# A list of instructions ordered by new ranks: lengths of ScalarE's pieces, ranks of pairs and weights' pieces, and an output tile of its own for the last half

## The chip, the cores and the metric

The kernel runs on 1 core of one Trainium2 chip. The metric is the device time of one execution in microseconds (us), lower is better. The engines are named PE (TensorE, matmuls), DVE (VectorE), ACT (ScalarE), POOL (GpSimd) and SP (SyncE, which here only issues DMAs).

## What is computed

Block-causal attention over 8 batches of 8 heads, 576 positions and 64 features, and behind it a gated feed-forward layer on all 4608 tokens. Cut to what matters:

```python
# q, k, v: (8, 8, 576, 64); blocks of 64 positions, a query sees its own and earlier blocks
scores = q @ k.transpose(0, 1, 3, 2) / sqrt(64)
scores = where(block_i >= block_j, scores, -1e9)
attn = exp(scores - scores.max(-1, keepdims=True))
attn = attn / (attn.sum(-1, keepdims=True) + 1e-9)
x = (attn @ v).transpose(0, 2, 1, 3).reshape(4608, 512)
g = x @ w_gate                       # (512, 1536)
out = (g * sigmoid(g) * (x @ w_val)) @ w_out      # (1536, 512), fp32 out
```

The weights arrive as 64-bit floats, as two 32-bit words each.

## The kernel before

**The work and its pieces.** The attention goes by pairs of heads: four pairs to a batch. Batches 0 and 1 are cut into tokens 0 to 255 and 256 to 575 (the table FIRST), so that the feed-forward of the first 256-token tiles can begin early; later batches go whole. For one pair PE makes scores (L429 for the first two batches after transposes L403; L555 with operands in high and low parts for the others, whose low part DVE makes at L523). ACT copies scores out of PSUM (L447, L473, L565) and hides what a block may not see (L452, L470). DVE takes the maximum over keys (L603), POOL reduces it over partitions (L607), DVE subtracts it (L631), ACT takes the exponential (L635), and PE multiplies with v (L675). In batch 0 DVE divides at once, out of PSUM (L702 to L709).

A feed-forward tile holds 256 tokens. Every value goes as a high and a low part, so that each product is three matmuls: L998 to L1000 for gate and value (into PSUM tiles gv), L1089 to L1091 for the output (into po or at). Between them ACT takes a tanh (L1031), DVE multiplies (L1034, L1039), ACT makes the high part (L1044) and DVE the low one (L1047). At a tile's end ACT copies the sums out (L1116) and SP stores them. In the very last 128 tokens the row is halved: DVE copies the second half (L1114), and ACT's queue stores it.

The weights come in 36 pieces (12 of each of w_gate, w_val, w_out). Each is loaded into one of five buffers wo, turned from 64-bit to 32-bit words by ACT and DVE (L857, L861, L866, L871), and split into a high part by ACT (L876) and a low part by DVE (L879).

**What sets the order.** Nothing is issued where it is written. `add(engine, cost, rank, fn, after, bufs)` records a task with an estimated length, a rank, what it comes after, and the buffers it needs. When all tasks are recorded, `in_order` (L1184 and below) goes through them as a list scheduler does: each engine takes, of the tasks that are ready, the one with the lowest rank, if its buffers can be had; `spare` says how long before an engine is free a buffer may have come free. A task's end follows from its cost, so the costs decide the order too. The tasks are then issued in the order found, and each engine works its own line strictly in that order. The times in the scheduler are estimates of its author and appear nowhere else.

The ranks are numbers written out by hand: PIECES (one for each piece of the weights), AHEAD (for the loads of the first pieces), FIRST (pairs of the first two batches), LEAD (how far ahead of the feed-forward a later batch goes), SIDE (the first two feed-forward tiles), EAGER (how far the scores go ahead of the rest of a pair) and MIXED (how the sixths of the first two tiles follow each other). `act_us` gives the cost of a piece of ACT's work, 0.08 us and 0.000833 us for each column.

Of the kernel before, what the change touches and what calls it, by code (L numbers as in the profile page):

```python
# [18 lines left out]
def kernel(  # L19
# [19 lines left out]
    NT, DM = out.shape  # L39
# [3 lines left out]
    TB = 96  # L43
# [6 lines left out]
    XT = 256  # L50


    LEAD, EAGER = 1.88, 0.3

    SUMS = 2

    MIXED = (0, 0, 0, 1, 1, 0, 1, 0, 1, 0, 1, 1)

    FINE = 4

    AHEAD = {(0, 1): 2.01, (0, 2): 2.03, (1, 0): 2.5, (1, 1): 2.07, (1, 2): 2.07}
    LATER = 0.6

    PIECES = [
        (2.64, 2.64, 2.71),
        (2.85, 3.37, 2.76),
        (5.12, 5.12, 4.37),
        (4.66, 4.68, 4.68),
        (2.95, 3.91, 4.11),
        (4.18, 4.18, 4.91),  # L70
        (4.71, 4.38, 4.79),
        (2.20, 2.82, 2.82),
        (1.32, 1.14, 0.01),
        (1.91, 1.85, 2.33),
        (0.26, 1.61, 0.56),
        (2.08, 2.78, 1.84),
    ]

    SIDE = (3.40, 10.26)

    PATIENCE = 10.0

    FIRST = {
        0: [(0, 256, (2.02, 2.21, 2.06, 2.08)), (256, 576, (1.99, 2.09, 0.10, 2.03))],
        1: [(0, 256, (1.33, 2.46, 3.26, 3.40)), (256, 576, (1.79, 1.87, 2.05, 2.09))],
    }
    TILES = [XT] * (NT // XT)

# [70 lines left out]
        return t  # L159


    def act_us(n):
        return 0.08 + n * 0.000833

    def dve_us(n, one=False):
        return 0.07 + n * (0.00052 if one else 0.00104)
# [167 lines left out]
    def attention(R, b, h, a, e, early, bufs, lane):  # L334
# [1 line left out]

        Q = R - (0.001 if early else EAGER)
        visits, runs = STRETCHES[a, e]  # L340
        if b < 2:

# [27 lines left out]
        def plain_scores():  # L370
# [21 lines left out]
            for i in range(2):  # L392
                ps = Buf("gv") if whole else Buf("at", also=banks)
                nb = len(blocks[i])
                per = nb if nb < 6 else 3

                def turned(ps=ps):
                    return ps[0].rearrange("p (x n) -> p x n", x=1) if whole else ps[0]

                def transposes(i=i, turned=turned, per=per):  # L400
                    for m, c in enumerate(blocks[i]):
                        o = m % per * TB
                        nc.tensor.transpose(  # L403
                            turned()[:, m // per, o : o + TB],
                            qk[0][:TB, lane * 3 + c, 2 * i * D : 2 * (i + 1) * D],
                            ident[:TB, :TB],
                        )

                def out_of_psum(i=i, turned=turned, nb=nb, per=per):
                    o = L + blocks[i][0] * TB  # L410
                    nc.scalar.mul(
                        prt[i][:, o : o + nb * TB].rearrange("p (x n) -> p x n", x=nb // per),
                        turned()[:, 0 : nb // per, 0 : per * TB],
                        1.0 if i else SCALE,
                    )

                tr = add("PE", 0.083 * nb, R, transposes, [ld[i]], [qk, ps, prt])
                ready.append(add("ACT", act_us(nb * TB), R, out_of_psum, [tr], [ps, prt]))

            for visit in visits:  # L420
                both = [Buf("at", also=banks) for _ in visit]
# [18 lines left out]
                for parts, ps in zip(visit, both):  # L440
                    gw = sum(w for _, _, w in parts)
                    mixed = [(c, sum(w for _, _, w in parts[:i])) for i, (c, qs, _) in enumerate(parts) if qs == c * P]

                    def out_of_psum(parts=parts, ps=ps, gw=gw):
                        c, qs, _ = parts[0]
                        o = place[c] + qs - first[c]
                        nc.scalar.copy(sc[0][:, :, o : o + gw], ps[0][:, :, 0:gw])  # L447

                    def hide(mixed=mixed, ps=ps):

                        for c, o in mixed:
# [12 lines left out]

                    if whole:
                        stays.append(ps)

                        def hide_there(ps=ps):
                            x = ps[0].rearrange("p x (n w) -> p x n w", w=2 * P)[:, :, :, 0:BLK]
                            nc.scalar.activation(x, x, AF.Identity, bias=unseen)  # L470

                        def max_there(ps=ps):
                            nc.scalar.copy(mx[0][:, :, L : L + W], ps[0][:, :, 0:W])  # L473

                        t = add("ACT", act_us(4 * BLK) + 0.1, Q, hide_there, [pr], [ps])
                        t = add("ACT", act_us(2 * W), Q, max_there, [t], [ps, mx])
                        evac[0].append(t)
                        evac[1].append(t)
                        continue
                    t = add("ACT", act_us(2 * gw), Q, out_of_psum, [pr], [ps, sc])  # L480
                    if mixed:
                        t = add("ACT", 0.28 * len(mixed), Q, hide, [t], [ps, sc])
                    if parts[0][:2] == (0, 0):
                        t = add("ACT", 0.46, Q, first_max, [t], [ps, mx])
                    for c, _, _ in parts:
                        evac[c].append(t)

        def split_scores():
# [48 lines left out]
            for x in range(2):  # L537
                for group in (((0, 0, half), (0, half, half)), ((1, 4), (2, 3))):
# [42 lines left out]
                    t = add("ACT", act_us(2 * gw), Q, out_of_psum, [pr], [ps, sc])  # L581
# [105 lines left out]
        for i, s0, s1, _ in pieces:  # L687

            def out_of_psum(i=i, s0=s0, s1=s1):
                nc.scalar.copy(xu[0][:, L + s0 + here - a : L + s1 - a], ps[0][:, i, here : s1 - s0])  # L690

            if s1 - s0 > here:
                ends.append(add("ACT", act_us(s1 - s0 - here), R, out_of_psum, [pr], [ps, xu]))

        if here:
            xt, xhl = Buf("xt"), Buf("xhl")
# [14 lines left out]
            t = add("DVE", 1.2, 1.0, invert, [pr], [ps, sr, xt])  # L711
# [54 lines left out]
        if direct:  # L766
# [4 lines left out]
            sm = [add("ACT", act_us(W - here), R, sums_there, [pr], [ps, sr])] * 2  # L771
# [40 lines left out]
    def weight(i, kind):  # L812
# [68 lines left out]
            )  # L881

        if wide:
            t = add("ACT", act_us(DM), R, signs, [t], [raw, y])
            f = add("DVE", dve_us(DM), R, fraction, [t], [raw, y], True)
            t = add("ACT", act_us(DM), R, scaled, [t], [raw])
            t = add("DVE", dve_us(DM), R, exponent, [t, f], [raw], True)
        t = w_high[i, kind] = add("ACT", act_us(DM), R, high, [t], bufs)
# [75 lines left out]
    def feed_forward(j, t0, w, xs):  # L964
# [50 lines left out]
        for i in range(0, NFC, 2):  # L1015
# [32 lines left out]
                    hh[1][:, 0:n], t[0][:, 0:n], hh[0][:, 0:n].bitcast(F32), ALU.subtract  # L1048
                )

            a = add("ACT", act_us(n), E, tanh, [tg], [pg, t])
            a = add("DVE", dve_us(n), E, silu2, [a], [pg, t])
            a = add("DVE", dve_us(n), E, gated, [a, tv], [pv, t])
            a = add("ACT", act_us(n), E, high, [a], [t, hh])
# [48 lines left out]
                yield  # L1103

        for m in range(nb):
            ob = Buf("ob", "out")

            halves = 2 if ends_alone and m == nb - 1 else 1
            for x in range(halves):
                cols = slice(x * DM // halves, (x + 1) * DM // halves)  # L1110

                def out_of_psum(m=m, ob=ob, x=x, cols=cols):
                    if x:
                        nc.vector.tensor_copy(ob[0][:, cols], sums(m)[:, cols])  # L1114
                    else:
                        nc.scalar.copy(ob[0][:, cols], sums(m)[:, cols])  # L1116
# [5 lines left out]
                us = (dve_us if x else act_us)(DM // halves)  # L1122
# [61 lines left out]
    def in_order():  # L1184
# [14 lines left out]
        now = queue = 0.0  # L1199
        mode, last = "", None  # L1200

        spare = {"PE": 2.0, "DVE": 0.3, "ACT": 0.3, "POOL": 0.0, "SP": 0.0}

        def place(t, by):

# [104 lines left out]
```

## Time and profile before

| what | us |
|---|---|
| median of 3 runs (1180.5 to 1184.99) | 1183.08 |
| the profiled execution, its own time | 1180.03 |
| span in the profile | 1178.2 |
| PE busy | 1148.2 |
| DVE busy | 768.9 |
| ACT busy | 635.9 |
| POOL busy | 324.9 |

An engine's busy time is that of its instructions; register, branch, semaphore and DMA-issuing ones aren't counted. Matmuls are pipelined, so one lasts longer (0.28 us for 256 columns) than the step from its start to the next one's start, which is what the sums use. A row of a wait names the waiting engine and line, what it waited for, and then total us, times and longest. A wait for several things is put down to the one that came last.

### The profile page before, as it was taken

Reading aid. Unit: us, or ns where it says so; the run is one execution under the profiler, and the core shown is the slowest. Engines: PE = TensorE matmul, PEld = TensorE weight load, DVE = VectorE, ACT = ScalarE, POOL = GpSimd, SP = SyncE. Lnnn points to the kernel's source line nnn. Section 1 sums busy time; section 2 is a strip of 40 time slices with the busy share of each in tenths; the row PEclk is TensorE's granted clock in tenths of the full one; section 3 lists DMA queues with packets and bytes.
Section 4 is the critical chain, followed back from the end, with each engine's and each line's share of the span. In section 5 each row is a group of like instructions: output and inputs, shape, how many; then the busy total and the mean of one; then the engine's idle time right before and its main releaser. Section 6 shows DMA issues by size and latency. Waiting matters only on the chain.

```text
span 1178.2 us, 21734 instructions
## 1 busy us (share of the span) xinstructions
PE 1148.2 (97%) x8464; PEld 1029.9 (87%) x8464; DVE 768.9 (65%) x1234; ACT 635.9 (54%) x1150; POOL 324.9 (28%) x138
## 2 busy tenths in 40 slices
PE   6889999999999999999999999999999999999998
PEld 4667777889898989898998999898989899999997
DVE  5998988876687667877585767675767633323222
ACT  6898967757574736574655556564746312212111
POOL 3122110143634162345233325243344300000000
PEclk9999999999999999999999999999999999999999
DMA  8778656755564746755656464646662445453432
GB/s 214 188 199 214 192 180 197 208 178 160 147 169 115 210 146 176 204 164 153 181 168 182 138 192 134 198 134 190 159 199 92 153 157 183 150 167 136 144 130 103
DMA packets 266983, 197.40 MB, mean 168 GB/s; under 512 B 195264, under 2 KB 231376, under 8 KB 266880
## 3 DMA queue, kind: packets, MB, share of 16 engines
q1 hardware_dynamic: 264304, 195.29, 56.8%
q8 instruction: 66, 1.08, 0.4%
q10 hardware_dynamic: 2576, 0.72, 0.3%
q14 instruction: 37, 0.30, 0.1%
HBM read 171.57 MB, written 24.38 MB: 166 GB/s over the span
## 4 chain that ended last, share of the span: by engine, by line
PE 84%; ACT 6%; DVE 5%; DMA 2%; POOL 1%; issue 1%; SPq 0%; ACTq 0%; DVEq 0%; POOLq 0%
PE gv L998 15%; PE gv L1000 15%; PE gv L999 15%; PE po L1089 7%; PE po L1090 7%; PE po L1091 7%; PE at L555 7%; PE at L675 7%; POOL mx L607 1%; DVE mx L603 1%; DVE sc L631 1%; ACT sc L447 1%; ACT ob L857 1%; ACT sc L635 1%; DVE wo L866 1%
## 5 line engine op out<-in xcount | busy, mean ns | idle before, releaser
L607 POOL PARTITION_ALL_REDUCE mx<-mx x80 | 144.6, 1855 | 405.7 <-DVE mx L603 192.6
L998 PE MATMUL gv<-xhl,v_all 128*128 128x256 f32 x864 | 241.5, 280 | 0.7 <-DVE t L1039 0.7
L1000 PE MATMUL gv<-xhl,v_all 128*128 128x256 f32 x864 | 239.4, 277 | 0.0
L999 PE MATMUL gv<-xhl,v_all 128*128 128x256 f32 x864 | 239.3, 277 | 0.0
L726 POOL PARTITION_ALL_REDUCE mx<-mx x48 | 178.1, 3758 | 205.8 <-DVE mx L603 205.8
L1034 DVE SCALAR_TENSOR_TENSOR t<-t,gv 128x512 f32<-128x512 f32 x108 | 74.0, 685 | 209.3 <-ACT t L1031 208.9
L998 PEld LDWEIGHTS gv<-xhl,v_all 128*128 128x128 f32 x864 | 162.1, 188 | 4.9 <-issue 2.7
L999 PEld LDWEIGHTS gv<-xhl,v_all 128*128 128x128 f32 x864 | 162.3, 188 | 0.9
L1000 PEld LDWEIGHTS gv<-xhl,v_all 128*128 128x128 f32 x864 | 162.2, 188 | 0.0
L1031 ACT ACTIVATE t<-gv 128x512 f32<-128x512 f32 x108 | 64.5, 598 | 169.5 <-PE gv L1000 169.4
L1089 PE MATMUL po<-wo,hhl 128*128 128x512 f32 x372 | 147.7, 397 | 0.3 <-ACT ob L1116 0.3
L1090 PE MATMUL po<-wo,hhl 128*128 128x512 f32 x372 | 145.6, 391 | 0.0
L1091 PE MATMUL po<-wo,hhl 128*128 128x512 f32 x372 | 145.1, 390 | 0.0
L1044 ACT CAST hhl<-t 128x512 fp32r<-128x512 f32 x108 | 67.2, 622 | 139.3 <-DVE t L1039 138.0
L631 DVE TENSOR_TENSOR sc<-sc,mx 128x640 f32<-128x640 f32 (+6 forms) x168 | 123.9, 773 | 18.5 <-POOL mx L607 18.3
L635 ACT ACTIVATE sc<-sc 128x1024 f32<-128x1024 f32 (+3 forms) x104 | 105.5, 1028 | 35.8 <-DVE sc L631 35.1
L998 PE MATMUL gv<-xhl,g_even 128*128 128x256 f32 x432 | 123.2, 285 | 0.1
L999 PE MATMUL gv<-xhl,g_even 128*128 128x256 f32 x432 | 122.3, 283 | 0.2 <-DVE xhl L326 0.2
L1000 PE MATMUL gv<-xhl,g_even 128*128 128x256 f32 x432 | 122.1, 283 | 0.0
L1039 DVE SCALAR_TENSOR_TENSOR t<-t,gv 128x512 f32<-128x512 f32 x108 | 73.9, 684 | 73.1 <-PE gv L1000 72.7
L998 PE MATMUL gv<-xhl,g_odd 128*128 128x256 f32 x432 | 120.7, 279 | 0.7 <-ACT g_odd L876 0.7
L1000 PE MATMUL gv<-xhl,g_odd 128*128 128x256 f32 x432 | 119.7, 277 | 0.6 <-DVE g_odd L879 0.6
(157 smaller groups left out, 2465.2 us busy)
## 6 DMA issues: line engine op xcount, KB each, us to landing
wo<-wo_d SPq DMA_DIRECT2D x200, 512.0 KB
out_dram<-ob SPq DMA_DIRECT2D x35, 256.0 KB
v<-in_v_dram SPq DMA_DIRECT2D x64, 128.0 KB
xt<-x_d SPq DMA_DIRECT2D x64, 128.0 KB
rt<-r_d SPq DMA_DIRECT2D x128, 64.0 KB
qk<-in_q_dram SPq DMA_DIRECT2D x112, 72.0 KB
qk<-in_k_dram SPq DMA_DIRECT2D x104, 72.0 KB
x_d<-xu SPq DMA_DIRECT2D x24, 288.0 KB
```

The lines of the kernel that those rows point to most:

```text
L555: nc.tensor.matmul(ps[0][:, i, o : o + w], lhsT=prt[x][1][:, c * P : (c + 1) * P], rhs=m, start=not low, stop=low == 1,)
L607: nc.gpsimd.partition_all_reduce(m, m, channels=P, reduce_op=bass_isa.ReduceOp.max)
L631: nc.vector.tensor_tensor(piece(c), scores_of(c), m, ALU.subtract)
L635: nc.scalar.activation(x, x, AF.Exp)
L675: nc.tensor.matmul(ps[0][own(x), 1 - i if sums else i, q0 - s0 : s1 - s0], lhsT=ones if sums else vt[0][:, 2 * lane + c, own(x)], rhs=sc[0 ...
L726: nc.gpsimd.partition_all_reduce(m, m, channels=P, reduce_op=bass_isa.ReduceOp.add)
L998: nc.tensor.matmul(o, lhsT=hi[:, d], rhs=xhi[:, 0:w], start=first, stop=False)
L999: nc.tensor.matmul(o, lhsT=hi[:, d], rhs=xlo[:, 0:w], start=False, stop=False)
L1000: nc.tensor.matmul(o, lhsT=lo[:, d], rhs=xhi[:, 0:w], start=False, stop=last)
L1089: nc.tensor.matmul(po, lhsT=hi, rhs=whi, start=i + y == 0, stop=False)
L1090: nc.tensor.matmul(po, lhsT=hi, rhs=wlo, start=False, stop=False)
L1091: nc.tensor.matmul(po, lhsT=lo, rhs=whi, start=False, stop=i + y == NFC - 1)
```

## The change

Three kinds of edits. The cost of an ACT piece gets other numbers: 0.093 us in place of 0.08, 0.05 where it reads PSUM, and something more for three kinds of weights' work; DVE's `invert` and ACT's `hide` get other costs too. The hand-written ranks get other values (all of PIECES, AHEAD, FIRST; also LEAD, SIDE, MIXED, the early EAGER, and `spare`). And the second half of the last 128 tokens takes a buffer of tag t instead of sharing the one of tag ob. What is computed, with which instructions and shapes, stays as it is. Of the tables two lines stand for all:

```diff
-    LEAD, EAGER = 1.88, 0.3
+    LEAD, EAGER = 1.85, 0.3
-    MIXED = (0, 0, 0, 1, 1, 0, 1, 0, 1, 0, 1, 1)
+    MIXED = (0, 0, 0, 1, 1, 0, 0, 1, 1, 1, 0, 1)
     PIECES = [
-        (2.08, 2.78, 1.84),
+        (-6.75, -4.32, -5.69),
...
-    def act_us(n):
-        return 0.08 + n * 0.000833
+    def act_us(n, psum=False, more=0.0):
+        return (0.05 if psum else 0.093) + n * 0.000833 + more
...
-        Q = R - (0.001 if early else EAGER)
+        Q = R - (0.1 if early else EAGER)
...
         for m in range(nb):
-            ob = Buf("ob", "out")
 
             halves = 2 if ends_alone and m == nb - 1 else 1
             for x in range(halves):
+                ob = Buf("t") if x else Buf("ob", "out")
...
-        spare = {"PE": 2.0, "DVE": 0.3, "ACT": 0.3, "POOL": 0.0, "SP": 0.0}
+        spare = {"PE": 1.59, "DVE": 0.30, "ACT": 0.75, "POOL": 0.0, "SP": 0.0}
```

What moves is seen in the lines of the engines. First, ACT at the start of the program: loads of k (qk), the load of its function tables (L1142), copies of transposed q and k (parts), and the first scores (at) and their copy (mx). Before:

```order
L1142 ACT_TABLE_LOAD
L1142 ACTIVATE seen<-seen 128x1
L379 DMA qk_0_124<-in_k_dram 96x3x64 x2
L379 DMA qk_0_127<-in_k_dram 96x3x64 x4
L411 ACTIVATE parts_0_148<-gv_0_138 128x288
L379 DMA qk_0_124<-in_k_dram 96x3x64 x2
L411 ACTIVATE parts_1_149<-gv_0_154 128x288
L470 ACTIVATE at_0_164<-at_0_164,unseen 128x4x64
L411 ACTIVATE parts_0_148<-gv_0_138 128x288
L473 COPY mx_0_178<-at_0_164 128x2x256
```

Now:

```order
L379 DMA qk_0_123<-in_k_dram 96x3x64 x2
L1142 ACT_TABLE_LOAD
L1142 ACTIVATE seen<-seen 128x1
L379 DMA qk_0_133<-in_k_dram 96x3x64 x4
L379 DMA qk_0_123<-in_k_dram 96x3x64 x2
L411 ACTIVATE parts_0_155<-gv_0_142 128x288
L411 ACTIVATE parts_1_156<-gv_0_148 128x288
L470 ACTIVATE at_0_164<-at_0_164,unseen 128x4x64
L473 COPY mx_0_174<-at_0_164 128x2x256
L411 ACTIVATE parts_0_155<-gv_0_142 128x288
```

Two loads went ahead of the table load, two ahead of the first L411, and L473 ahead of the next pair's L411.

Second, DVE at one of the maxima in batch 1 (sc_0_291 the scores of a pair, mx_0_245 or mx_0_241 their maximum, which POOL reduces between the last L603 and the first L631; wo and g are weights). Before:

```order
L879 TENSOR_TENSOR wo_0_1572<-wo_0_96,wo_0_1572 128x512
L603 TENSOR_TENSOR mx_0_245<-mx_0_245,sc_0_291 128x2x64
L603 TENSOR_TENSOR mx_0_245<-mx_0_245,sc_0_291 128x2x320
L631 TENSOR_TENSOR sc_0_291<-sc_0_291,mx_0_245 128x2x320
L631 TENSOR_TENSOR sc_0_291<-sc_0_291,mx_0_245 128x2x192
```

Now:

```order
L603 TENSOR_TENSOR mx_0_241<-mx_0_241,sc_0_291 128x2x320
L879 TENSOR_TENSOR wo_0_1552<-wo_0_98,wo_0_1552 128x512
L866 SCALAR_TENSOR_TENSOR wo_0_95<-wo_0_95,ob_0_260 128x512
L955 TENSOR_TENSOR xt_0_271<-xt_0_271,rt_0_1544 128x256
L871 SCALAR_TENSOR_TENSOR wo_0_95<-wo_0_95 128x512
L631 TENSOR_TENSOR sc_0_291<-sc_0_291,mx_0_241 128x2x320
```

Four rows of other work came between the last L603 and L631, where there were none.

Third, PE at the first score matmuls of batch 2 (L555; wo, g and v_all are weights, hhl and xhl the feed-forward's tokens). Before:

```order
L1089 MATMUL at_0_164<-wo_0_1911,hhl_0_99 128x512
L1090 MATMUL at_0_164<-wo_0_1911,hhl_0_99 128x512
L1091 MATMUL at_0_164<-wo_0_1911,hhl_1_100 128x512
L998 MATMUL gv_0_154<-xhl_0_86,g_even_76 128x256
L999 MATMUL gv_0_154<-xhl_1_87,g_even_76 128x256
L1000 MATMUL gv_0_154<-xhl_0_86,g_even_77 128x256
L555 MATMUL at_0_199<-qk_0_1949,parts_1_1959 128x288
```

Now:

```order
L998 MATMUL gv_0_148<-xhl_0_86,v_all_73 128x256
L999 MATMUL gv_0_148<-xhl_1_87,v_all_73 128x256
L1000 MATMUL gv_0_148<-xhl_0_86,v_all_74 128x256
L555 MATMUL at_0_199<-qk_0_1926,parts_1_1937 128x288
L555 MATMUL at_0_199<-parts_0_1936,parts_1_1937 128x288
L555 MATMUL at_0_199<-qk_0_1926,parts_1_1937 128x288
L555 MATMUL at_0_199<-parts_0_1936,parts_1_1937 128x288
L1089 MATMUL at_0_164<-wo_0_1688,hhl_0_99 128x512
```

Output matmuls that stood ahead of batch 2's first scores stand behind them.

More of the change, by code (lines that the diff above doesn't have):

```diff
@@ L50 @@
     XT = 256
[L53 removed]
+    LEAD, EAGER = 1.85, 0.3
     SUMS = 2
[L57 removed]
+    MIXED = (0, 0, 0, 1, 1, 0, 0, 1, 1, 1, 0, 1)
     FINE = 4
[L61 removed]
+    AHEAD = {(0, 1): 2.07, (0, 2): 2.05, (1, 0): 2.03, (1, 1): 2.5, (1, 2): 2.07}
     LATER = 0.6
     PIECES = [
[L65 to L75, printed above, removed]
[L76 removed]
+        (2.64, 1.21, 2.65),
+        (3.96, 5.41, 4.06),
+        (5.14, 3.10, 2.72),
+        (4.84, 3.88, 6.04),
+        (2.32, 3.36, 2.32),
+        (6.15, 7.45, 7.22),
+        (3.67, 2.81, 3.57),
+        (-0.33, -0.09, 1.99),
+        (-2.22, -5.25, -4.35),
+        (-3.17, -1.74, -0.17),
+        (-2.07, -3.47, -2.21),
+        (-6.75, -4.32, -5.69),
     ]
[L79 removed]
+    SIDE = (2.98, 10.13)
     PATIENCE = 10.0
     FIRST = {
[L84 to L85 removed]
+        0: [(0, 256, (-1.41, 2.61, 2.06, 2.08)), (256, 576, (1.23, 2.12, -3.94, 0.76))],
+        1: [(0, 256, (2.13, 1.84, 3.12, 2.24)), (256, 576, (-1.08, 0.53, 1.77, 2.89))],
     }
@@ L417, in plain_scores @@
                 tr = add("PE", 0.083 * nb, R, transposes, [ld[i]], [qk, ps, prt])
-                ready.append(add("ACT", act_us(nb * TB), R, out_of_psum, [tr], [ps, prt]))
+                ready.append(add("ACT", act_us(nb * TB, True), R, out_of_psum, [tr], [ps, prt]))
             for visit in visits:
@@ L479, in plain_scores @@
                         continue
-                    t = add("ACT", act_us(2 * gw), Q, out_of_psum, [pr], [ps, sc])
+                    t = add("ACT", act_us(2 * gw, True), Q, out_of_psum, [pr], [ps, sc])
                     if mixed:
-                        t = add("ACT", 0.28 * len(mixed), Q, hide, [t], [ps, sc])
+                        t = add("ACT", 0.245 * len(mixed), Q, hide, [t], [ps, sc])
                     if parts[0][:2] == (0, 0):
@@ L580, in split_scores @@
                     pr = add("PE", us, Q, products, ready[x], [ps, high, prt[x], sc])
-                    t = add("ACT", act_us(2 * gw), Q, out_of_psum, [pr], [ps, sc])
+                    t = add("ACT", act_us(2 * gw, True), Q, out_of_psum, [pr], [ps, sc])
                     t = add("ACT", 0.5 if gw == 512 else 0.2, Q, hide, [t], [ps, sc])
@@ L692, in attention @@
             if s1 - s0 > here:
-                ends.append(add("ACT", act_us(s1 - s0 - here), R, out_of_psum, [pr], [ps, xu]))
+                ends.append(add("ACT", act_us(s1 - s0 - here, True), R, out_of_psum, [pr], [ps, xu]))
         if here:
@@ L709, in divide @@
                 nc.vector.tensor_tensor(xt[0], ps[0][:, i, 0:here], xt[0], ALU.mult)
-            t = add("DVE", 1.2, 1.0, invert, [pr], [ps, sr, xt])
+            t = add("DVE", 1.3, 1.0, invert, [pr], [ps, sr, xt])
             t = add("DVE", dve_us(here), 1.0, divide, [t], [ps, xt])
@@ L769, in sums_there @@
                 nc.scalar.copy(sr[0][:, L + here : L + W], ps[0][:, 1 - i, here:W])
-            sm = [add("ACT", act_us(W - here), R, sums_there, [pr], [ps, sr])] * 2
+            sm = [add("ACT", act_us(W - here, True), R, sums_there, [pr], [ps, sr])] * 2
             total = lambda x0, x1: sr[0][x0 * D : x1 * D : D, :]
@@ L883, in weight @@
         if wide:
-            t = add("ACT", act_us(DM), R, signs, [t], [raw, y])
+            t = add("ACT", act_us(DM, more=0.13), R, signs, [t], [raw, y])
             f = add("DVE", dve_us(DM), R, fraction, [t], [raw, y], True)
-            t = add("ACT", act_us(DM), R, scaled, [t], [raw])
+            t = add("ACT", act_us(DM, more=0.06), R, scaled, [t], [raw])
             t = add("DVE", dve_us(DM), R, exponent, [t, f], [raw], True)
-        t = w_high[i, kind] = add("ACT", act_us(DM), R, high, [t], bufs)
+        t = w_high[i, kind] = add("ACT", act_us(DM, more=0.04), R, high, [t], bufs)
         t = add("DVE", dve_us(DM), R, low, [t], bufs, True)
@@ L1049, in low @@
                 )
-            a = add("ACT", act_us(n), E, tanh, [tg], [pg, t])
+            a = add("ACT", act_us(n, True), E, tanh, [tg], [pg, t])
             a = add("DVE", dve_us(n), E, silu2, [a], [pg, t])
@@ L1120, in store @@
                     (nc.scalar if x else nc.sync).dma_start(out=out[r0 : r0 + P, cols], in_=ob[0][:, cols])
-                us = (dve_us if x else act_us)(DM // halves)
+                us = dve_us(DM // halves) if x else act_us(DM // halves, True)
                 e = add("DVE" if x else "ACT", us, E, out_of_psum, [ends[m]], [accs[m], ob])
```

## The prediction

> **What bounds the kernel now.** I read the page first, then the busy time of each engine by stage, then who waited for whom in each stage, then single rows at the places where the change acts. The page's totals and slices:
>
> ```profile
> span 1178.2 us, 21734 instructions
> ...
> PE 1148.2 (97%) x8464; PEld 1029.9 (87%) x8464; DVE 768.9 (65%) x1234; ACT 635.9 (54%) x1150; POOL 324.9 (28%) x138
> ...
> PE   6889999999999999999999999999999999999998
> ...
> DVE  5998988876687667877585767675767633323222
> ACT  6898967757574736574655556564746312212111
> ```
>
> TensorE is busy 97% of the span. DVE and ACT are full only in the first five or so slices, where PE shows its 6 and 8s. The same by stage, with columns of start and end, then busy time of PE, weight loads, DVE, ACT and POOL, PE's granted clock, and DMA:
>
> ```profile
> 0.00:24.00 24.00, 14.76 (x92) 11.27 (x94) 11.72 (x37) 13.53 (x28) 9.18 (x16) 0.93 0.84 206
> 24.00:100.00 76.00, 65.02 (x510) 48.83 (x506) 69.75 (x136) 68.41 (x133) 19.08 (x14) 0.96 0.72 194
> 100.00:200.00 100.00, 97.20 (x710) 77.69 (x711) 89.02 (x155) 79.29 (x144) 16.74 (x12) 1.00 0.67 198
> 200.00:344.00 144.00, 140.62 (x1027) 127.84 (x1026) 103.95 (x157) 92.38 (x166) 51.70 (x18) 1.00 0.61 172
> 344.00:1174.60 830.60, 830.60 (x6133) 764.23 (x6131) 494.05 (x752) 381.92 (x682) 228.22 (x78) 1.00 0.54 160
> ```
>
> PE idles 9.2 us up to 24, 11.0 up to 100, 2.8 up to 200 and 3.4 up to 344: 26.4 in all. From 344 to its last matmul it never stops. So an order of work can win only in the first 344 us. There DVE is the engine PE follows: it is busy 69.75 of 76 and 89.02 of 100, that is, it idles 6.25 + 10.98 = 17.2 us between 24 and 200. PE's waits end on ACT and DVE; the two longest from 24 to 200 (total, times, longest):
>
> ```profile
> PE at L403 <- ACT parts L411: 2.3, 2, 2.1
> PE at L429 <- ACT parts L411: 1.8, 1, 1.8
> ```
>
> and one from the stretch 200 to 344:
>
> ```profile
> PE at L555 <- DVE parts L523: 1.5, 3, 1.0
> ```
>
> The first of its three waits is the gate of which I speak below: the first matmul of batch 2's scores stands in PE's line until DVE has made its operand.
>
> **The change, part by part.** No instruction is added or taken away on PE, DVE or POOL; ACT keeps its 1150 too. The new lengths and ranks act through the order alone, so each term is a place where the order differs.
>
> *The start.* ACT's first rows before:
>
> ```profile
> 0.73 1.28 ACT L1142 ACT_TABLE_LOAD   x1 [0.73 <-PEq L1293]
> 1.18 0.92 ACTq L379 DMA_DIRECT2D qk<-in_k_dram  x2
> 2.02 0.20 ACT L1142 ACTIVATE seen<-seen 128x1 f32<-128x1 f32 x1
> 2.13 2.45 ACTq L379 DMA_DIRECT2D qk<-in_k_dram  x4
> 5.13 0.87 ACTq L379 DMA_DIRECT2D qk<-in_k_dram  x2
> 6.04 0.41 ACT L411 ACTIVATE parts<-gv 128x288 f32<-128x288 f32 x1 [0.90 <-DMA qk<-in_k_dram]
> ```
>
> Two k loads now go ahead of the table load, and all eight ahead of the first L411. The table load then starts after two issues of 0.46 (0.92 for two), at about 1.65, and ends 1.28 later at 2.9, so the third and fourth loads go out some 0.8 later than at 2.13. The last issue waits for the fourth load to land, and behind it on ACT stand both L411, for which PE's first scores wait: 0.8 later. Against that, ACT's copy L473, for which DVE's maximum and POOL's reduction wait, no longer stands behind the next pair's L411 (0.41). That leaves 0.4; the second pair's L473 has one more piece of ACT ahead of it, so I take **+0.5**, bounds 0 (the loads were early enough anyway) and +0.9 (nothing comes back). DVE has idled 12.3 of the first 24 us and is nearly full behind, so what the start loses is carried on.
>
> *The maxima on POOL.* DVE subtracts a maximum (L631) after POOL has reduced it; what DVE has to do between its last L603 and that L631 hides the reduction. DVE's waits from 24 to 200, first two rows, and two of POOL's reductions:
>
> ```profile
> DVE sc L631 <- POOL mx L607: 7.7, 5, 2.7
> DVE wo L866 <- ACT ob L857: 2.1, 2, 1.5
> ```
> ```profile
> 113.72 2.47 POOL L607 PARTITION_ALL_REDUCE mx<-mx  x2 [3.86 <-DVE mx L603]
> 159.65 2.47 POOL L607 PARTITION_ALL_REDUCE mx<-mx  x2 [17.73 <-DVE mx L603]
> ```
>
> A pair of reductions takes 2.47, about 2.7 with the hand-overs of some 0.1 on both sides. I counted the DVE work that stands in each of the 13 gaps up to 200, each row at the mean of its shape in this trace. Short of 2.7 are, before, gaps by 0.65, 0.9, 0.7, 1.05, 1.25, 0.9, 0.1, 2.7 and 0.6, together 8.85, of which the row above shows 7.7; the 2.7 is the gap with nothing in it. After, they are short by 0.95, 0.75, 0.55, 0.25, 1.25, 0.4, 0.4 and 1.4: 5.95. The difference of 2.9, scaled by 7.7 / 8.85, is **-2.5**. Bounds: 0, if DVE then waits for ACT instead, and -7.7, if all of it goes.
>
> *The gate at batch 2.* DVE's rows before it, and its last row, which ends PE's wait:
>
> ```profile
> 197.98 0.68 DVE L1047 TENSOR_TENSOR hhl<-t,hhl 128x512 fp32r<-128x512 f32 x1
> 198.58 0.68 DVE L1034 SCALAR_TENSOR_TENSOR t<-t,gv 128x512 f32<-128x512 f32 x1
> ...
> 199.78 0.17 DVE L928 TENSOR_SCALAR st<-st 128x16 f32<-128x16 f32 x1
> 199.98 0.25 DVE L929 RECIPROCAL st<-st 128x16 f32<-128x16 f32 x1
> ...
> 200.81 1.54 DVE L523 TENSOR_TENSOR parts<-sr,parts 64x576 fp32r<-64x576 f32 x2
> ```
> ```profile
> 201.71 0.37 PE L555 MATMUL at<-qk,parts 128*128 128x288 f32 x1
> ```
>
> Ahead of the L523 for which that first L555 waits, DVE's line now holds one L1034, one L1047, one L928 and one L929 less: 0.68 + 0.68 + 0.17 + 0.25 = 1.8. Ahead of the L555 itself PE's line holds 153 triples of L998 to L1000 instead of 157 and 32 of L1089 to L1091 instead of 36. What one of these takes is seen from a run of each, where starts follow by 0.12 and 0.23:
>
> ```profile
> 108.34 0.12 PE gv L998
> ...
> 1169.83 0.23 PE at L1089
> ```
>
> Twelve of each kind are 12 x 0.12 + 12 x 0.23 = 4.2 us. If DVE has idled as long as before, the gate opens 1.8 earlier and 4.2 more stand behind it: **+2.4**. At the last such gate of batch 2, 36 matmuls of L555 later, the same count gives +1.7, so this isn't given back at once. Bounds: 0, where PE fills up with work that it reaches elsewhere, and +4.2, where DVE doesn't come earlier.
>
> *The end.* The second half of the last 128 tokens goes to a tile of its own. The rows before:
>
> ```profile
> 1174.64 0.42 DVE L1114 COPY ob<-at 128x256 f32<-128x256 f32 x1 [3.39 <-PE at L1091]
> 1175.10 0.37 ACT L1116 COPY ob<-at 128x256 f32<-128x256 f32 x1 [1.23 <-DVE ob L1114]
> ```
>
> Were the halves free of each other, ACT would start at 1174.64 too, 0.46 earlier. In the changed program ACT's copy still waits for DVE's last one, since both read the same PSUM tile: **0**, bounds -0.46 and 0. [...]
>
> Sum: 0.5 - 2.5 + 2.4 + 0 = +0.4 us. The profiled execution took 1180.03 us (span 1178.2), and the median of the three runs is 1183.08, 3.05 above it: 1180.4 for a run like the profiled one, **1183.5** as a median. A measurement here can tell about 0.5%, or 5.9 us, from no change.
>
> **The rivals.**
>
> *Faster: DVE's waits go.* If all 7.7 us of waits for POOL go instead of 2.5, and the 2.1 for ACT's L857 (these waits are what truer ACT lengths should place better), it is 5.2 + 2.1 = 7.3 less: 1176.2. For it speaks that the empty gap of 2.7 is filled; against it, that eight of 13 gaps are still short by count. It decides from the point at which DVE's wait for POOL falls under 1 us.
>
> *Slower: PE stands in front of one DVE row.* In batch 1's first 256 tokens, PE's L429 into tile po waits for DVE's L709 to read po. In the new order that L709 is DVE's 138th instruction, and 288 matmuls stand ahead of the L429. In the old order DVE began its 138th at 78.66, and PE had done as much work when it came to a L429 at 74.42:
>
> ```profile
> 78.66 0.68 DVE L1034 SCALAR_TENSOR_TENSOR t<-t,gv 128x512 f32<-128x512 f32 x1
> ```
> ```profile
> 74.42 0.98 PE L429 MATMUL at<-parts,parts 64*128 64x320 f32 x8
> ```
>
> PE would be 4.2 us late there. I expect it to catch up by not standing in the waits that the old order has from there to 200. If it doesn't, and DVE and ACT wait for PE in their turn so that the 2.5 of POOL's gaps are lost as well, it is +6.7: 1190.2. It decides when the first L555 starts at 201 or later, 3 us behind the forecast's 198 (below). The clock would add to it: PE was granted 0.96 of it between 24 and 100. [...]
>
> *It does nothing that shows.* The gates stay where they are and the order only permutes hidden work: 1183.1. This lies within my forecast.
>
> **How the numbers follow.** The forecast, a change inside 0.5%, has 0.54; the faster rival 0.25; the slower one 0.21. The range takes in both rivals' prices: below, 1176.2 less the end's 0.46, 1175.7; above, 1190.2, which the bounds of start and gate don't pass (0.9 + 4.2 without the 2.5 is 1188.2). So faster by over 0.5% 0.25, within 0.5% 0.54, slower by over 0.5% 0.21.
>
> **What would show it.** Right: ACT's second L411 starts about 6.8 instead of 6.04; DVE's wait for POOL between 24 and 200 reads about 5 instead of 7.7; the first L555 starts near 198 (201.7 - 1.8 - 2.5 + 0.5 = 197.9), with fewer matmuls ahead of it; PE still never idles from about 344 on; ACT's last copy still begins after DVE's. Wrong: a first L555 before 195 or after 201, a new wait of PE over 3 us near 80, or PE idling after 344, which nothing in the order leads me to expect.

## The result and the profile after

| what | before | after |
|---|---|---|
| median of 5 runs, us | 1182.51 (1180.36 to 1184.99) | 1189.6 (1186.99 to 1192.49) |
| the profiled execution, its own time | 1180.03 | 1186.99 |
| span in the profile | 1178.2 | 1185.0 |

The ratio is 1.0059, 95% interval 1.0037 to 1.008: 7.1 us slower, a little more than the 0.5% that was set as the limit of no change, and the interval takes in that limit. One of the 12 executions of e2_pool below took 6446.52 us and is left out of its ratio. The page of the changed kernel, span, busy times, and the slices of PE and of its granted clock:

```profile
span 1185.0 us, 21746 instructions
...
PE 1150.3 (97%) x8464; PEld 1033.1 (87%) x8464; DVE 766.7 (65%) x1234; ACT 636.6 (54%) x1150; POOL 328.3 (28%) x138
...
PE   7789889999999999999999999999999999999998
...
PEclk9989999999999999999999999999999999999999
```

The same work is done, and PE is still 97% busy. By stage (start and end, busy time of PE, weight loads, DVE, ACT and POOL, PE's granted clock, DMA):

```profile
0.00:24.00 24.00, 16.14 (x86) 12.15 (x88) 11.53 (x37) 14.40 (x29) 8.82 (x16) 1.00 0.82 202
24.00:100.00 76.00, 66.17 (x514) 48.69 (x512) 68.50 (x134) 66.25 (x129) 18.32 (x14) 0.93 0.69 186
100.00:200.00 100.00, 89.81 (x669) 72.89 (x666) 86.01 (x149) 77.49 (x141) 17.72 (x12) 1.00 0.66 196
200.00:344.00 144.00, 140.99 (x1024) 127.75 (x1023) 104.84 (x158) 94.50 (x169) 51.06 (x18) 1.00 0.63 174
344.00:1181.40 837.40, 837.12 (x6184) 771.64 (x6182) 495.37 (x758) 383.56 (x685) 232.36 (x78) 1.00 0.54 159
```

The loss sits in one row: between 100 and 200 PE now idles 10.2 us, where it idled 2.8. That is 7.4; the three other rows up to 344 idle 2.9 less together, PE's busy time is 2.1 longer in all, and the span is 6.8 longer. All three engines idle more in that row: DVE is 3.0 less busy than before, ACT 1.8. Of the waits that the prediction counted on, DVE's between 24 and 200, the first three rows:

```profile
DVE wo L866 <- ACT ob L857: 4.6, 5, 2.0
DVE sc L631 <- POOL mx L607: 3.0, 2, 2.0
DVE t L1039 <- PE gv L1000: 3.0, 3, 2.1
```

The wait for POOL's maxima fell from 7.7 to 3.0, more than forecast, and DVE still idles longer in all: its idle time in these 176 us is 7.5 + 14.0 = 21.5, where it was 17.2. So the time saved in that row came up again in others. Where PE stood, and what ACT did just before it (PE's two longest waits of the stretch, and two rows of ACT):

```profile
113.09 0.92 PE L429 MATMUL at<-parts,parts 64*128 64x256 f32 x8 [2.09 <-ACT parts L411]
...
170.75 2.28 PE L675 MATMUL at<-sc,v 128*64 128x320 f32 x20 [2.67 <-ACT sc L452]
```
```profile
111.93 0.77 ACT L857 ACTIVATE ob<-wo 128x512 f16<-128x512 f32 x1 [2.77 <-DMA wo<-in_moe_w_out_dram]
...
167.19 0.79 ACT L857 ACTIVATE ob<-wo 128x512 f16<-128x512 f32 x1 [2.51 <-DMA wo<-in_moe_w_val_dram]
```

ACT stands in front of a weights' piece whose load has not landed, and the work that PE waits for stands behind that piece. In all, ACT's waits for loads in this stage:

```profile
ACT ob L857 <- DMA wo<-in_moe_w_out_dram: 3.6, 3, 2.8
...
ACT ob L857 <- DMA wo<-in_moe_w_gate_dram: 2.8, 1, 2.8
ACT ob L857 <- DMA wo<-in_moe_w_val_dram: 2.5, 1, 2.5
```

That is 8.9 us, where before it was 4.1. This gave the first theory.

### The profile page after: what moved, and what is told of

It is laid out like the page before. It is cut to its first block, busy times and chain, and to the rows that moved or that the text cites. A ratio compares the mean times of both kernels' runs of the same rounds, so it can differ in the third digit from the quotient of the medians.

```text
span 1185.0 us, 21746 instructions
## 1 busy us (share of the span) xinstructions
PE 1150.3 (97%) x8464; PEld 1033.1 (87%) x8464; DVE 766.7 (65%) x1234; ACT 636.6 (54%) x1150; POOL 328.3 (28%) x138
## 4 chain that ended last, share of the span: by engine, by line
PE 69%; ACT 1%; DVE 1%; DMA 1%; issue 0%; SPq 0%
PE gv L998 13%; PE gv L1000 13%; PE gv L999 13%; PE po L1089 6%; PE po L1090 6%; PE po L1091 6%; PE at L555 5%; PE at L675 5%; PE at L1090 0%; PE at L1089 0%; PE at L1091 0%; DMA r_d<-st 0%; DMA rt<-r_d 0%; DVE parts L523 0%; ACT sc L635 0%; ACT sc L565 0%
## 5 line engine op out<-in xcount | busy, mean ns | idle before, releaser
L607 POOL PARTITION_ALL_REDUCE mx<-mx x80 | 146.3, 1877 | 402.7 <-DVE mx L603 128.6
L998 PE MATMUL gv<-xhl,v_all 128*128 128x256 f32 x864 | 241.1, 279 | 0.0
L1000 PE MATMUL gv<-xhl,v_all 128*128 128x256 f32 x864 | 239.6, 277 | 0.0
L726 POOL PARTITION_ALL_REDUCE mx<-mx x48 | 179.7, 3791 | 197.3 <-DVE mx L603 182.3
L998 PEld LDWEIGHTS gv<-xhl,v_all 128*128 128x128 f32 x864 | 162.1, 188 | 2.8 <-issue 1.5
L1000 PEld LDWEIGHTS gv<-xhl,v_all 128*128 128x128 f32 x864 | 162.2, 188 | 0.0
L631 DVE TENSOR_TENSOR sc<-sc,mx 128x640 f32<-128x640 f32 (+6 forms) x168 | 127.1, 796 | 18.2 <-POOL mx L607 17.9
L998 PE MATMUL gv<-xhl,g_even 128*128 128x256 f32 x432 | 123.1, 285 | 1.7 <-DVE t L1039 1.0
L1000 PE MATMUL gv<-xhl,g_even 128*128 128x256 f32 x432 | 122.1, 283 | 0.0
L998 PE MATMUL gv<-xhl,g_odd 128*128 128x256 f32 x432 | 121.1, 280 | 0.0
L1000 PE MATMUL gv<-xhl,g_odd 128*128 128x256 f32 x432 | 120.2, 278 | 0.0
```

Of the source, the lines that this page charges most:

```text
L607: nc.gpsimd.partition_all_reduce(m, m, channels=P, reduce_op=bass_isa.ReduceOp.max)
L631: nc.vector.tensor_tensor(piece(c), scores_of(c), m, ALU.subtract)
L726: nc.gpsimd.partition_all_reduce(m, m, channels=P, reduce_op=bass_isa.ReduceOp.add)
L998: nc.tensor.matmul(o, lhsT=hi[:, d], rhs=xhi[:, 0:w], start=first, stop=False)
L1000: nc.tensor.matmul(o, lhsT=lo[:, d], rhs=xhi[:, 0:w], start=False, stop=last)
```

## The experiments

**Theory one, the loads:** the new ranks of the weights put L857 ahead of loads that land late. **Rivals:** the maxima (DVE's waits for POOL set the pace), and the early gates (what PE loses before 100, above all in front of L709 near 80, is what stays lost). The idle time of PE and its granted clock, from the rows by stage of each run's one profiled execution, with time and ratio to before (executions of before in the same session, whose medians are 1182.23 to 1182.55):

| kernel | median us | ratio, 95% interval | PE idle 24 to 100 | clock there | PE idle 100 to 200 |
|---|---|---|---|---|---|
| before | 1182.51 | 1 | 11.0 | 0.96 | 2.8 |
| after | 1189.6 | 1.0059, 1.0037 to 1.008 | 9.8 | 0.93 | 10.2 |
| e1_stands | 1186.4 | 1.0033, 1.0015 to 1.0051 | 11.9 | 0.96 | 7.7 |
| e2_pool | 1188.84 | 1.0044, 1.0025 to 1.0063 | 10.8 | 0.92 | 10.2 |
| e3_after_old_pieces | 1189.04 | 1.0055, 1.0037 to 1.0072 | 13.1 | 0.87 | 10.2 |
| e4_before_new_pieces | 1192.38 | 1.0076, 1.0048 to 1.0104 | 12.4 | 0.86 | 4.2 |
| e5_gate | 1189.78 | 1.0059, 1.0044 to 1.0075 | 10.2 | 0.93 | 9.5 |
| e6_all | 1189.09 | 1.0057, 1.0044 to 1.0069 | 9.7 | 0.90 | 8.4 |
| e7_lengths | 1232.84 | 1.0416, 1.0397 to 1.0436 | 12.3 | 0.86 | 7.1 |
| e8_ranks | 1192.76 | 1.0079, 1.0062 to 1.0096 | 11.6 | 0.86 | 3.9 |
| e9_after_eager | 1185.81 | 1.0019, 1.0006 to 1.0032 | 10.8 | 0.93 | 4.1 |
| e10_before_spare | 1192.18 | 1.0078, 1.0057 to 1.01 | 14.8 | 0.84 | 3.9 |
| e11_before_refit | 1181.56 | 0.9991, 0.9977 to 1.0005 | 10.0 | 0.95 | 2.4 |
| e12_after_refit | 1181.99 | 0.9985, 0.997 to 1.0 | 10.5 | 0.90 | 4.2 |

### Three places in the new order

In these runs the order of the changed kernel is kept as found, and single tasks are put behind others (tasks by their number of creation; `behind(m, n)` puts n right behind m).

e1_stands, the two L857 with what hangs on them:

```diff
+    behind(380, 1930)
+    behind(445, 2011, 2013, 2012)
```

> The changed kernel with its order kept, except that two of ScalarE's pieces L857 which stood 2.77 us (at 111.93) and 2.51 us (at 167.19) for a load of weights go behind the work that stood behind them (one L411; one L447 and two L635). Theory of the loads: TensorE's waits of 2.09 at 113.09 and 2.67 at 170.75 go, since nothing else is late there; 4.8 us less, 1189.6 becomes about 1185, TensorE idles some 5.5 us between 100 and 200 instead of 10.2. Rival, the maxima: VectorE's waits for GpSimd set the pace, TensorE waits as long for something else a little later: within 1 us of 1189.6. Rival, the early gates: what is lost before 100 us is lost and the rest is scatter: within 1 us too.

Measured: 1186.4, some 3 of the 4.8. PE's waits of 0.6 and more between 105 and 175:

```profile
112.73 0.56 PE L403 MATMUL at<-ident,qk 96*128 96x96 f32 x4 [1.38 <-ACT parts L411]
...
140.13 0.43 PE L734 MATMUL at<-sc,ones 128*64 128x128 f32 x3 [0.98 <-ACT parts L411]
...
145.01 0.81 PE L429 MATMUL at<-parts,parts 64*128 64x320 f32 x4 [1.70 <-ACT sc L452]
...
167.14 2.28 PE L675 MATMUL at<-sc,v 128*64 128x320 f32 x20 [0.77 <-ACT sc L452]
```

The wait of 2.67 fell to 0.77. The one of 2.09 did not go: PE now stands 1.38 at the next thing that ACT has to hand over. A place that is freed lets the next one show.

e2_pool, DVE's L631 that waited 2.01 for POOL:

```diff
+    behind(1950, 302)
```

> The changed kernel with its order kept, except that VectorE's one L631 that waited 2.01 us for GpSimd's L607 at 127.46 goes behind an L603 and an L879 that stood behind it. Theory of the loads: VectorE's wait falls by about 1.3, TensorE's 0.91 at 129.04 goes, and no more: 1188 to 1189.6. Rival, the maxima: this wait is what ScalarE's 2.50 at 129.86 and TensorE's 1.01, 0.58 and 1.71 between 141 and 147 come from: 3 to 4 us less, about 1186.

Measured: 1188.84, ratio 1.0044 beside 1.0059, inside each other's intervals. The rival's 3 to 4 us are not there, and PE idles as long as in the changed kernel. DVE's L631 no longer waits at this place. The maxima alone don't carry the loss; a gain of a microsecond can't be told from none.

e5_gate, the place of the prediction's slower rival:

```diff
+    behind(2467, 247)
+    behind(195, 196)
```

> The changed kernel with its order kept, except at the place near 80 us: TensorE's one L429 into po, which waited 2.38 us for VectorE's L709, goes behind one piece of L403 and two triples of L998 to L1000, and that L709 goes ahead of the one L603 and one L871 that stood before it. Theory of the early gate: the wait falls from 2.4 to about 0.5, and the slow stretch behind it (triples that step by 0.21 instead of 0.12 up to 85) goes as well; 3 to 4 us less, about 1186. Rival: ScalarE and VectorE did not stand at this place, and set when the rest comes; TensorE waits for them a little later instead: within 1 us of 1189.6.

Measured: 1189.78, nothing gained. PE's row at this place in the changed kernel, and in this run:

```profile
79.64 0.92 PE L429 MATMUL po<-parts,parts 64*128 64x256 f32 x8 [2.38 <-DVE xt L709]
```
```profile
79.94 0.47 PE L403 MATMUL at<-ident,qk 96*128 96x96 f32 x3 [1.85 <-ACT sc L452]
```

PE no longer waits for L709; at the same moment it waits for ACT's L452, in front of the L403 that now comes first. By these two rows the place had two reasons to wait that came almost together, and the trace names only the last.

e6_all, the three moves together.

> The changed kernel with the three moves together: ScalarE's L857 at 112 and 167, VectorE's L631 at 127 and TensorE's L429 at 80. If the stands add up: 3.1 of the first run, 1.5 of the second and what the third gives, 1182 to 1185, so the loss is these places. Rival: each place that is freed lets the next one come late, and the three together give no more than the first alone: 1186 to 1187.

Measured: 1189.09, ratio 1.0057. The places don't add up, and even the 3 us of e1_stands, whose moves are in this kernel too, are not found again. So no single stand, nor these three, is the loss; I count e1_stands as open.

### Parts of the change

e3_after_old_pieces and e4_before_new_pieces exchange the ranks of the weights alone:

```diff
-        (-6.75, -4.32, -5.69),
+        (2.08, 2.78, 1.84),
```

> The changed kernel with PIECES and AHEAD, the ranks of the weights, as they were before; lengths, pairs' ranks and the rest stay changed. Theory of the loads: the weights' pieces no longer go first on ScalarE, waits of L857 for its loads between 100 and 200 fall from 8.9 to about 4, and the time falls to 1181 to 1185. Rival, the maxima, or the early gates: lengths and pairs' ranks set them, the time stays at 1187 to 1191.

> The kernel before with only PIECES and AHEAD of the changed one. Theory of the loads: ScalarE stands for loads between 100 and 200 by 8 us or more instead of 4.1, and the time is 1187 to 1191. Rivals: 1181 to 1184, as before.

Measured: 1189.04 and 1192.38. Theory one would have the second without the first: the new ranks cost 9 us in the old order, but taking them back in the new one brings nothing. Nor does ACT's waiting for loads between 100 and 200 go with the time: it is 4.6 in e3_after_old_pieces and 6.7 in e4_before_new_pieces, beside 8.9 in the changed kernel and 4.1 before. By themselves the new ranks of the weights are not the part that costs. PE's longest wait before 100 in e3_after_old_pieces is at an L709 (the sixth of DVE's; the prediction's rival spoke of the seventh), and in e4_before_new_pieces at an L452:

```profile
71.39 1.44 PE L429 MATMUL po<-parts,parts 64*128 64x320 f32 x4 [5.39 <-DVE xt L709]
```
```profile
74.31 1.44 PE L429 MATMUL at<-parts,parts 64*128 64x320 f32 x4 [4.52 <-ACT sc L452]
```

So a second theory, **the fit:** ranks and lengths were chosen together, by trial; no part is good or bad by itself, and the change lost because its whole is fitted a little worse. **Rival:** the lengths, or the ranks, are at fault in themselves. e7_lengths and e8_ranks take one half each:

```diff
-    def act_us(n):
-        return 0.08 + n * 0.000833
+    def act_us(n, psum=False, more=0.0):
+        return (0.05 if psum else 0.093) + n * 0.000833 + more
...
-        spare = {"PE": 2.0, "DVE": 0.3, "ACT": 0.3, "POOL": 0.0, "SP": 0.0}
+        spare = {"PE": 1.59, "DVE": 0.30, "ACT": 0.75, "POOL": 0.0, "SP": 0.0}
```

(e7_lengths; e8_ranks has the ranks of the change and keeps these lines as they were.)

> The new lengths and spare alone, with all ranks as they were before (the last half's tile apart, as in the change). Theory that lengths and ranks belong together: the ranks were chosen by hand for the old lengths, so the new ones alone move pairs and weights against each other and TensorE stands long somewhere before 200; slower than the changed kernel, 1192 or more. Rival, the lengths are better in themselves and the new ranks are what costs: 1178 to 1184.

> The new ranks (PIECES, AHEAD, FIRST, MIXED, SIDE, LEAD, the early EAGER) with the lengths and spare of before. Theory that lengths and ranks belong together: new ranks without their lengths lose as well, 1186 to 1194. Rival, the ranks alone make the difference and the lengths change little: within 1.5 us of 1189.6; second rival, the ranks are good and the lengths cost: 1178 to 1184.

Measured: 1232.84 and 1192.76. Lengths that differ by 0.01 to 0.15 us a piece, with `spare`, cost 4.2% when the ranks aren't chosen for them. Some 19 to 30 of the 50 us are lost past 344 (two stages, and PE's first row of waits there):

```profile
344.00:400.00 56.00, 45.10 (x310) 39.08 (x308) 39.74 (x62) 35.34 (x62) 22.64 (x8) 0.91 0.51 133
400.00:450.00 50.00, 42.04 (x286) 37.75 (x286) 33.84 (x47) 24.15 (x46) 23.51 (x8) 0.87 0.47 127
```
```profile
PE gv L998 <- ACT xhl L323: 7.5, 2, 4.3
```

PE idles 10.9 and 8.0 there, and the clock of 0.91 and 0.87 takes at most another 5.0 and 6.5 (part of it falls on time in which PE idles): a feed-forward tile stands in PE's line before its tokens are there. The lengths alone are far slower than the whole; the ranks alone have 1.0079 beside its 1.0059, and their intervals overlap.

### One number, and ranks chosen anew

e9_after_eager takes back a single number of the change:

```diff
-        Q = R - (0.1 if early else EAGER)
+        Q = R - (0.001 if early else EAGER)
```

> The changed kernel with one number as it was before: the early EAGER 0.001 instead of 0.1, so that a pair's scores go only just ahead of the rest of the pair. Theory of the fit (the order as a whole is worse fitted, and no single place is the cause): one number that orders pairs anew moves the time by several us; by the stands that I can follow in the new order 2 to 5 less, 1184.5 to 1187.5. Rival, the loss is in the new lengths: within 1 us of 1189.6.

Measured: 1185.81, ratio 1.0019: 3.8 us less than the changed kernel by the medians, more than half of the loss. PE idles 4.1 between 100 and 200 instead of 10.2, and yet the waits of the first theory and of the maxima are there (this run's row of the stage; ACT's waits from 100 to 200 and DVE's from 24 to 200, the rows for loads and for POOL):

```profile
100.00:200.00 100.00, 95.89 (x688) 77.30 (x685) 86.56 (x148) 78.05 (x139) 18.22 (x12) 0.98 0.69 207
```
```profile
ACT ob L857 <- DMA wo<-in_moe_w_out_dram: 5.2, 4, 1.8
ACT ob L857 <- DMA wo<-in_moe_w_val_dram: 2.7, 1, 2.7
ACT ob L857 <- DMA wo<-in_moe_w_gate_dram: 1.3, 2, 0.7
```
```profile
DVE sc L631 <- POOL mx L607: 6.1, 5, 2.0
```

ACT stands 9.2 us for loads here, and 8.9 in the changed kernel; DVE stands 6.1 for POOL, twice as long as there. So neither wait has a price of its own, and the first theory falls. What the number does to the order is seen where the two orders part. Up to about 136 us all engines run the same rows; then, on ACT (- the changed kernel, + this one):

```
 L857 ACTIVATE ob_0_207<-wo_0_95 128x512
+L1031 ACTIVATE t_0_511<-gv_0_142 128x512
 L452 ACTIVATE sc_0_215<-at_0_199,unseen 128x2x64
-L1031 ACTIVATE t_0_511<-gv_0_142 128x512
```

The pair whose scores these are has the rank 0.53, the feed-forward's tanh 0.501. With 0.001 the scores stand at 0.529, behind the tanh; with 0.1 at 0.43, ahead of it. From there the orders differ everywhere. Between 136 and 172 PE is busy 29.3 of 36 us in the changed kernel, 34.0 here, 35.7 before. But these two executions can't say what the parting is worth. The last row that they share on ACT, in the changed kernel and in this one:

```profile
135.61 0.81 ACT L857 ACTIVATE ob<-wo 128x512 f16<-128x512 f32 x1
```
```profile
132.75 0.81 ACT L857 ACTIVATE ob<-wo 128x512 f16<-128x512 f32 x1
```

This run is 2.9 us ahead there, after the same rows on every engine: that is scatter between executions, and it is more than the 2.4 by which the whole spans differ (1185.0 and 1182.6). What PE idles less behind the parting is given back, partly at a lower clock (0.95 between 136 and 172), partly by idling 4.0 us between 344 and 1179. That the number is worth this much is shown by the medians; where the 3.8 us lie, these traces don't show, and that the parting row is what costs is only argued.

e10_before_spare goes the other way, one number into the kernel before:

```diff
-        spare = {"PE": 2.0, "DVE": 0.3, "ACT": 0.3, "POOL": 0.0, "SP": 0.0}
+        spare = {"PE": 2.0, "DVE": 0.3, "ACT": 0.75, "POOL": 0.0, "SP": 0.0}
```

> The kernel before with one number of the change: spare of ScalarE 0.75 instead of 0.3, so that a task of ScalarE may take its turn 0.75 us before its buffer is free. Theory of the fit: one such number, without the ranks chosen for it, costs as much as the whole change: 1186 to 1191. Rival, single numbers matter little and only the whole of ranks or lengths does: 1181 to 1183.5.

Measured: 1192.18, 9.6 us slower than before, more than the whole change. PE's longest wait is again at the place near 74 that stood out in e4_before_new_pieces. These two and e8_ranks are slow in another stage than the changed kernel, ahead of 100: the clock of 0.84 to 0.86 instead of 0.96 alone is worth at most 7.6 to 9.1 of these 76 us (less by what falls on PE's idle time), and 100 to 200 is nearly as good as before.

```profile
73.91 0.90 PE L429 MATMUL at<-parts,parts 64*128 64x320 f32 x2 [4.61 <-ACT sc L452]
```

e11_before_refit and e12_after_refit keep the lengths of before and of after, and get some 20 other ranks each (e12_after_refit with e9's number too). A line of each table stands for the rest:

```diff
-        0: [(0, 256, (2.02, 2.21, 2.06, 2.08)), (256, 576, (1.99, 2.09, 0.10, 2.03))],
+        0: [(0, 256, (1.41, 2.21, 2.06, 2.08)), (256, 576, (1.99, 2.08, -0.34, 2.42))],
...
-        1: [(0, 256, (2.13, 1.84, 3.12, 2.24)), (256, 576, (-1.08, 0.53, 1.77, 2.89))],
+        1: [(0, 256, (2.26, 2.23, 3.18, 3.51)), (256, 576, (-0.10, 0.53, 1.88, 2.89))],
```

> The kernel before with its lengths and 19 of its ranks chosen anew, so that the order still comes out short when every piece but the matmuls is up to a tenth longer or shorter and a load lands half a us later than assumed. Theory of the fit: before is not the end of it, 2 to 4 less: 1178 to 1180.5. Rival: before stands where TensorE's first 344 us can't be shortened by order: within 1.5 us of 1182.3.

> The changed kernel with all its new lengths, the early EAGER of before, and some 20 of its ranks chosen anew in the same way. Theory of the fit: the lengths are not at fault, ranks that fit them give back most of the 7 us: 1182.5 to 1186. Rival, the new lengths hold TensorE back whatever the ranks: 1187 to 1190.

Measured: 1181.56 and 1181.99. The first missed what the theory expected and came out as its rival had it: 0.9991 with 1 in its interval, no gain that shows. The second gives back all 7 us, and a little more than was expected: with all the new lengths the kernel is as fast as before (0.9985, up to 1.0). So the lengths are not at fault in themselves; the ranks and the early EAGER that went with them are. Its stages from 24 to 200, and its longest wait in them:

```profile
24.00:100.00 76.00, 65.47 (x515) 46.68 (x512) 67.48 (x134) 65.46 (x131) 18.96 (x14) 0.90 0.66 177
100.00:200.00 100.00, 95.77 (x693) 76.94 (x691) 91.67 (x156) 82.92 (x147) 15.84 (x12) 1.00 0.73 213
```
```profile
70.83 1.44 PE L429 MATMUL at<-parts,parts 64*128 64x320 f32 x4 [3.42 <-DVE xt L709]
```

PE waits 3.42 in front of an L709 there (the sixth of DVE's again), longer than the changed kernel does in front of any, and is granted 0.90 of its clock instead of 0.93, and the kernel is 7.6 faster all the same. What PE lost early was won back in the next stage, where DVE is busy 91.67 of 100 and the changed kernel's reaches 86.01. With e5_gate this speaks against the early gate as the cause: a longer wait of its kind stands in a fast kernel, and taking the gate out of a slow one doesn't make it fast. What remains open is which of the ranks make up the second half, from e9_after_eager's 1185.81 to 1181.99; it was changed in some 20 numbers at once.

## Why the prediction was wrong where it was wrong

**What bounds the kernel** was right: PE idles 0.3 us between 344 and 1181.4, and the loss of 6.8 in the span lies before that.

**The start**, +0.5, was not there. ACT's row of its first two L411:

```profile
5.51 0.71 ACT L411 ACTIVATE parts<-gv 128x288 f32<-128x288 f32 x2 [2.28 <-DMA qk<-in_k_dram]
```

Both are done at 6.22. Before, the second began at 6.04 and ended at 6.45, and I had expected it to begin about 6.8. The table load moved by 1 us as counted, but the load that is waited for landed no later for it. Up to 24 PE even idles 1.4 less than before.

**The maxima on POOL**, -2.5: the wait fell even more, by 4.7. The step that failed is the one behind it, that DVE's time is PE's time, so that a wait taken from one row of DVE shortens the span. In the changed kernel the other rows of DVE grew by 9.0 (21.5 idle less 3.0, against 17.2 less 7.7), and e9_after_eager is faster with twice that wait. The faster rival, whose sign was a wait under 1 us, did not come.

**The gate at batch 2**, +2.4, was no gate any more. The first L555 starts at 204.5, and PE, which came later itself, doesn't wait there at all; fewer matmuls ahead of it and a DVE that is 1.8 earlier had nothing left to act on. By the sign that the prediction set (a first L555 at 201 or later) the slower rival had come true, and a first L555 after 201 was among the prediction's signs of being wrong.

**The end**, 0, was right, as are the two rows of it:

```profile
1181.47 0.42 DVE L1114 COPY t<-at 128x256 f32<-128x256 f32 x1 [3.40 <-PE at L1091]
```
```profile
1181.93 0.37 ACT L1116 COPY ob<-at 128x256 f32<-128x256 f32 x1 [1.23 <-DVE t L1114]
```

An output tile of its own leaves the two copies in one PSUM tile, and ACT's begins 0.46 after DVE's, as before: its wait of 1.23 still ends on DVE's L1114. That the PSUM tile which both read keeps them apart is my reading of one pair of rows; no run gives them two.

**The slower rival** named 1190.2, and 1189.6 was measured, but its mechanism is not the reason. The wait in front of L709 was there (2.38 instead of 4.2), and without it (e5_gate) the time stayed. Nor was PE late by then: up to 100 it had been busy 82.3 us, where it was 79.8 before, and it falls behind only after 100. That the price fits is chance, and it is this price that put 1189.6 inside the range.

**The chances:** 0.21 stood on slower by over 0.5%. The sum of +0.4 was made of places that the order shows to differ, and the stretch where PE idles most, 6.7 us between 136 and 172, was not among them: I had compared the orders at gates that I knew from the old trace, and a new order makes new ones.

## What to carry to other kernels

In this kernel, whose order a list of ranks and lengths makes, no number had a price of its own: one EAGER was worth 3.8 us, one `spare` 9.6 in the kernel before, and new lengths and `spare` without their ranks 50, while e12_after_refit has that `spare` and those lengths and is as fast as before. So judge such a change by the whole new order, stage by stage, and when lengths are corrected, choose the ranks again until the time is no longer than it was. And a wait in the trace is not a saving: move it away, and look whether the engine stands at the next row for another reason before it is counted. Before a difference between two traces is read, look how far apart they are where both still run the same rows: here it was 2.9 us.

## What the runs showed of the hardware

Up to 344, PE's granted clock falls to 0.50 three times in the changed kernel, at 33.01, 60.32 and 80.80, for 3.41 us each. These falls begin 27.31 and 20.48 us apart, eight and six times 3.41; in the kernel before, those at 17.50, 44.81 and 85.77 lie eight and twelve times 3.41 apart. They come after some stretches with little work, and not after others that hold as long a wait. The changed kernel, around its waits between 54 and 60 (the longest 1.23) and at 79.64 (2.38), in steps of 3.41 us:

```profile
56.91:60.32 3.41, 1.31 (x10) 0.93 (x11) 3.41 (x7) 3.41 (x9) 0.00 (x0) 1.00 0.69 209
60.32:63.73 3.41, 3.41 (x17) 1.71 (x17) 3.41 (x7) 3.38 (x8) 0.34 (x1) 0.50 0.87 233
77.39:80.80 3.41, 1.16 (x12) 1.07 (x12) 3.31 (x10) 3.41 (x9) 0.00 (x0) 1.00 0.56 172
80.80:84.21 3.41, 3.41 (x19) 3.41 (x18) 2.43 (x4) 2.27 (x7) 2.61 (x2) 0.50 0.67 188
```

Behind each, PE is granted 0.50 of its clock for 3.41 us (from 81.5 on, L998 to L1000 follow by 0.21 there, where a run of them near 108 before had 0.12). As an estimate, half of 3.41, that takes up to 1.7 us on top of the 2.1 and 2.25 that PE idled in the step before. Behind the wait of 2.67 at 170.75 and that of 2.09 at 113.09 the clock stays at 1.00. In the same steps, counted on from 80.80 (no fall marks them there), the wait of 2.67 is cut in two:

```profile
166.15:169.56 3.41, 1.92 (x17) 1.72 (x15) 1.85 (x4) 2.37 (x4) 0.00 (x0) 1.00 0.48 164
169.56:172.97 3.41, 2.22 (x21) 1.37 (x21) 3.39 (x6) 3.41 (x8) 0.00 (x0) 1.00 0.00 0
172.97:176.38 3.41, 3.41 (x22) 3.05 (x21) 3.41 (x7) 2.18 (x5) 0.00 (x0) 1.00 0.55 151
```

So here the clock fell behind steps with 1.31 and 1.16 us of work and not behind steps with 1.92 and 2.22. This is no threshold: in the kernel before it fell at 44.81, behind a step with 1.98, and in the changed one it stays at 1.00 from 5.70 to 9.12, behind a step with 1.22. Why one wait of 2.4 is followed by a fall and another of 2.7 is not, these traces don't show.

One load of weights was slower than the order assumes. In the lines of the list (`dma` and `in_order`), one of 512 KB has landed 0.65 + 1.48 + 0.9 = 3.0 us after its issue ends, if no other load is queued ahead of it. The one that ACT waited for at 167.19 was issued at 161.17:

```profile
161.17 0.43 SPq L842 DMA_DIRECT2D wo<-in_moe_w_val_dram  x1
```

That is 5.6 us from the issue's end. It fits that ACT waits in front of L857 for loads between 100 and 200, 4.1 us before, 8.9 in the changed kernel and 9.2 in e9_after_eager; a list with the true time of a load wasn't tried.
